# A recurrence in chunks of 64 tokens, its Gram products, triangular inverses and order rebuilt, ahead of a top-1 mixture of experts

## The chip, the cores and the metric

One core of one Trainium2 chip runs the whole program. The metric is the device time of one execution in microseconds. Before the change it is 550.36 us, the median of 3 runs (550.04 to 550.71).

The engines have one instruction stream each: TensorE (PE, matmuls), VectorE (DVE), ScalarE (ACT), GpSimd (POOL) and SyncE (SP, which only issues DMAs here). Each works through its stream in order and waits for the others at semaphores. PSUM banks take the products of TensorE, and ACT or DVE carry them on.

## The reference

Attention is a delta rule. For each of 4 batches and 8 heads a state of 48 by 48 runs over 768 tokens:

```python
k_n = k / (np.linalg.norm(k, axis=-1, keepdims=True) + 1e-06)
for t in range(S):
    kt, vt, bt = (k_n[:, :, t], v[:, :, t], beta[:, :, t, None])
    y[:, :, t] = np.einsum('bhd,bhde->bhe', q[:, :, t], state)
    v_old = np.einsum('bhde,bhd->bhe', state, kt)
    state = state + bt[:, :, :, None] * np.einsum('bhd,bhe->bhde', kt, vt - v_old)
```

Its output, as 3072 tokens of 384 numbers, goes through a mixture of 8 experts (384 to 1024 to 384):

```python
logits = x @ w_gate + modality_bias[modality_id]
e_idx = np.argmax(logits, axis=1)
# gate_w: the softmax of the chosen expert
h = np.maximum(x[mask] @ w1[e], 0.0)
out[mask] = gate_w[mask, None] * (h @ w2[e])
```

All is float32. The experts multiply float32 as a rounded high part and the rest, three products in place of one.

## The kernel before, in words

**Attention.** The 768 tokens are cut into 12 chunks of 64, the 32 batch-head pairs into two groups of 16, so there are 24 group steps i = 2c + g. Inside a chunk the recurrence is solved as a triangular system. Each step needs:

- the Gram products of its keys with its keys, and of its keys with its queries (method gram, L124). Keys are laid into a block-diagonal tile KB of 112 x 128, copied there by ACT and DVE, and 8 matmuls give four blocks of 32 keys and 64 queries each;
- the inverse of the triangular matrix. The 32 x 32 blocks on its diagonal are inverted for four steps at once, a set: 6 sets of 128 matrices, a matrix on each partition, by elimination: for each column a multiplication L213 and a subtraction L214, on DVE for the first 12 rows (sp1) and on POOL for the rest. Set 0 is done in blocks of 16, all on DVE, and joined by small products (jo, L247 and L253). Sets 0 and 1 stay on the chip; the others are carried through DRAM, both to bring blocks onto partitions and to bring the inverses back (R on L309, RTB on L305);
- level (L326, L330, L335, L338): the off-diagonal block of the inverse from two products, and the values scaled (L340, on POOL);
- chain: ks = state times keys (L363), RHS = values minus ks (L365, DVE), z = inverse times RHS (L378), ZT = z copied (ACT), state += keys times ZT (L386), Sbd = state copied (ACT), y = queries times state (L372) plus Gram times ZT (L394), xo = y copied (ACT), xd = xo written to DRAM (L397, SP);
- route: xo is transposed (L463), copied (L465) and multiplied by the gate's weights; each step writes 96 columns of one accumulating bank (L468).

Chain steps of one group follow on each other through the state; the two groups alternate.

**Routing and experts.** After 18 token tiles (step 17) part_a counts the tokens per expert, gives each a place (pt on TensorE, W, ranks, l0a and l1a one-hot tiles on DVE), sums the lists by matmuls (tpa) and copies them (tka, gidxa). SP reads the expert's number (sea) and loads its weights: w1 and w2 in four pieces each (w1ra, w2ra), which ACT rounds (w1ha, w2ha) and DVE takes the rest of (w1la, w2la). POOL gathers tokens from xd (xga), TensorE transposes them (xpa), ACT and DVE split them into x high and low. Layer 1 is hpa, layer 2 opa; POOL scatters the output rows (out_dram). The units in order are a0 to a3 (512 tokens each, from part_a's lists), b0 (512), c0 and c1 (256), e0 (128), whose lists part_b makes (tpb) from all 24 tiles. The order of all engines is found by the framework's scheduler from the written order and priorities, so a0's gather and first layer, and part_a, lie among steps 17 to 23.

## Time and profile before

| | before |
|---|---|
| median of 3 runs | 550.36 us |
| span of the profiled execution | 550.4 us |
| busy: PE, DVE, ACT, POOL | 483.5, 364.5, 263.5, 208.5 us |
| start of z of step 0, 4, 23 | 62.18, 131.68, 300.40 us |
| first product of a0's layer 1, of its layer 2 | 295.64, 317.71 us |
| start of the last scatter | 540.97 us |

The profiled execution's span is as long as a run, so its times can be set against the median as they are. Rows of a timeline have the start, the busy time (us), the engine, the line, the operation, output and input tiles and the count of instructions; in brackets the idle time ahead and what ended it. A float32 matmul shows as two records. PEclk is the clock that TensorE was granted, as a share of full speed.

### The profile page before, as it was taken

To read this page: it belongs to the slowest core of one execution; us is meant where nothing else is said; L and a number is where in the kernel's file an instruction comes from. 1 tells how busy PE (TensorE), PEld (TensorE's weight loads), DVE (VectorE), ACT (ScalarE), POOL (GpSimd) and SP (SyncE) were. 2 spreads that over 40 slices of the span, in tenths; PEclk is the share of its full clock that TensorE was granted. 3 is DMA by queue.
4 is the path that set the end of the run, shared out by engine and by line. 5 is a ranking of instruction groups with operands and counts; after the bars stand their busy time and mean duration, and the time that the engine had idled before them with its cause. 6 is when DMAs were issued, how large, how long until landed. Compare 5 with 4: busy or idle time off the path is not lost. (4 is left out here: it accounts for less than half of the span.)

```text
span 550.4 us, 14025 instructions
## 1 busy us (share of the span) xinstructions
PE 483.5 (88%) x5459; PEld 432.1 (79%) x5459; DVE 364.5 (66%) x877; ACT 263.5 (48%) x619; POOL 208.5 (38%) x350
## 2 busy tenths in 40 slices
...
GB/s 205 247 200 238 176 105 55 64 95 89 169 226 138 236 180 166 209 120 230 228 192 142 76 80 127 75 116 114 209 79 120 170 75 164 128 78 227 233 85 9
DMA packets 82716, 80.81 MB, mean 147 GB/s; under 512 B 50105, under 2 KB 73671, under 8 KB 81520
## 3 DMA queue, kind: packets, MB, share of 16 engines
...
q8 instruction: 45, 0.74, 0.6%
...
## 5 line engine op out<-in xcount | busy, mean ns | idle before, releaser
L733 PE MATMUL opa<-w2ha,h 128*128 128x384 f32 x256 | 69.1, 339 | 0.3 <-DVE ooa L736 0.3
L213 DVE TENSOR_TENSOR tm_x<-T,A 128x108 f32<-128x108 f32 (+12 forms) x165 | 57.8, 352 | 5.4 <-DVE PG L143 0.7
L124 PE MATMUL gp<-ke,KB 112*128 112x128 f32 x320 | 53.1, 331 | 9.3 <-DVE PG L143 3.9
L214 DVE TENSOR_TENSOR T<-T,tm_x 128x108 f32<-128x108 f32 (+12 forms) x165 | 56.8, 346 | 4.5
L124 PEld LDWEIGHTS gp<-ke,KB 112*128 112x128 f32 x320 | 48.3, 238 | 12.3 <-issue 3.7
L693 DVE SCALAR_TENSOR_TENSOR h<-hpa,h 128x512 fp32r<-128x512 f32 x32 | 22.0, 689 | 42.4 <-ACT h L692 42.4
L733 PEld LDWEIGHTS opa<-w2ha,h 128*128 128x128 f32 x256 | 46.2, 188 | 1.4 <-DVE ooa L736 0.5
L733 PE MATMUL opa<-w2la,h 128*128 128x384 f32 x128 | 43.0, 336 | 0.0
L692 ACT ACTIVATE h<-hpa 128x512 fp32r<-128x512 f32 x32 | 19.1, 596 | 49.5 <-PE hpa L690 49.5
L690 PE MATMUL hpa<-x,w1ha 128*128 128x512 f32 x144 | 39.1, 408 | 0.0
L340 POOL TENSOR_TENSOR kvn<-kvn,RR 128x384 f32<-128x384 f32 x22 | 18.7, 868 | 50.7 <-DMA kvn<-in_kv_dram 28.3
L363 PE MATMUL ks<-Sbd,kqr 112*64 112x96 f32 x352 | 27.3, 274 | 8.7 <-DMA kqr<-in_kq_dram 4.8
L365 DVE TENSOR_TENSOR RHS<-kvn,ks 64x384 f32<-64x384 f32 x44 | 24.2, 551 | 15.8 <-POOL kvn L340 9.4
L214 POOL TENSOR_TENSOR T<-T,tm_y 128x18 f32<-128x18 f32 (+8 forms) x90 | 30.7, 342 | 6.6
L213 POOL TENSOR_TENSOR tm_y<-T,A 128x18 f32<-128x18 f32 (+8 forms) x90 | 30.5, 339 | 6.6
L690 PEld LDWEIGHTS hpa<-x,w1ha 128*128 128x128 f32 x144 | 27.3, 194 | 5.5
L32 ACT COPY ZT<-z 64x384 f32<-64x384 f32 x48 | 22.7, 473 | 17.2 <-PE z L378 16.6
L363 PEld LDWEIGHTS ks<-Sbd,kqr 112*64 112x64 f32 x352 | 20.9, 150 | 11.8 <-ACT Sbd L32 4.4
L32 ACT COPY Sbd<-Sps 48x192 f32<-48x192 f32 x88 | 27.5, 313 | 5.2 <-PE Sps L386 2.7
L737 POOL DMA_INDIRECT out_dram<-ooa,sidxa x16 | 17.1, 1071 | 32.6 <-DMA out_dram<-ooa,sidxa 13.1
...
L378 PE MATMUL z<-RHS,R 128*64 128x96 f32 x384 | 26.9, 296 | 1.6 <-ACT R L338 1.6
...
## 6 DMA issues: line engine op xcount, KB each, us to landing
...
```

The costliest lines, as they stand in the source:

```text
L32: if n=="scalar": nc.scalar.copy(o,i)
L124: nc.tensor.matmul(gp[p][:,j,:],KB[:,x,:],k[:,x].rearrange("r a t -> r (a t)"),start=True,stop=True)
L213: yield I.tensor_tensor(o,y,z,ALU.mult)
L214: yield I.tensor_tensor(x,x,o,ALU.subtract)
L340: if c: E(C.vq).tensor_tensor(V,V,w,ALU.mult)
L363: nc.tensor.matmul(ks[64*p:64*p+64,:,j,:],KQ[:,4*p+j,0],hc(Sb[:,4*p+j,:]),start=True,stop=True)
L365: b=64*p; nc.vector.tensor_tensor(RH[b:b+64,:,48*p:48*p+48].rearrange("q (h j) c -> q h j c",h=2),VN[b:b+64],ks[b:b+64],ALU.subtract)
L378: s.PI['z',i]=nc.tensor.matmul(z[64*h:64*h+64,:,j,:],R[:,2*j+h,:],hc(RH[:,4*h+j,:]),start=True,stop=True)
L690: nc.tensor.matmul(hp[:,v,:],w[:,k,fs],x[:,k,0:T],start=(n==0),stop=(n==8)); n+=1
L692: nc.scalar.activation(hh,hp,AF.Relu)
L693: nc.vector.scalar_tensor_tensor(hl,hp,0.0,hh.bitcast(F32),ALU.max,ALU.subtract)
L733: mm=nc.tensor.matmul(op,h[:,f%nf,ts_],w[:,f%2,:],start=(n==0),stop=(n==23)); n+=1
```

## The change

- **Gram products in quadrants.** Keys and queries come without zeros, heads at partitions 0 and 64. A Gram of a chunk (both groups) is 32 matmuls of 48 rows, 64 columns out and 64 in (line 168), in all four quadrants of the array. Keys with keys (tiles gp0c, bank copies ev to gk) and keys with queries (gp1c, masked by DVE into pb) are two separate tasks. KB and its copies go, and the two matmuls at the start that multiplied nothing.
- **Set 0 first and in 16-blocks.** Its diagonal blocks are 32 x 32 products of their own (line 184) straight into a bank, then elimination of 15 columns on DVE as before, without key copies between.
- **Double sets.** JOBS is set 0, set 1, sets 2 and 3 together, sets 4 and 5 together. An instruction of a double job covers both sets (128 x 2 x ...). DVE has the first 8 rows of job 1 and the first 6 of jobs 2 and 3, POOL the rest; POOL also has the row scale and the final scale. Set 1 now goes through DRAM too, and the inverses come back by six small loads for each step from 4 on (rl, lines 348 and 351).
- **Logits by 32 columns.** The gate's weights are padded to 32 columns; for four tiles at once 12 matmuls give 32 rows each (line 529), ACT copies and DVE transposes.
- **xd is written by ACT's queue**, two DMAs a step.
- **Own list schedule.** The attention is a list of tasks with engine, duration, needs and buffers (class Plan). Latest times, backward from due times of z (T0 + PACE x i), are priorities; a simulation picks the order; in_order ties each engine to it.
- **Routing behind it.** part_a takes 20 tiles, is written after the whole attention, and a0's front and first layer may only issue after attention's last instruction on TensorE. List tiles come in rounds of 4 token tiles in place of 6. Expert buffers reuse those of the attention.

Three places in the instruction streams. First TensorE's start, the Grams of chunk 0's first step before:

```order
L124 MATMUL gp_0_122<-kqr_118,KB_112 128x128 [waits DMAHW0_49,DVE_49,Activation_49]
L124 MATMUL gp_0_122<-kqr_118,KB_112 128x128 x3
L124 MATMUL gp_1_127<-kqr_118,KB_112 128x128 x4
L124 MATMUL gp_1_150<-kqr_118,KB_113 128x128 [waits DMAHW1_49,Activation_49,Pool_49]
L124 MATMUL gp_1_150<-kqr_118,KB_113 128x128
```

and now, the diagonal blocks of step 2 and 3 and the Gram of chunk 0:

```order
L184 MATMUL S<-kqr_166 32x32 [waits DMAHW2_49]
L184 MATMUL S<-kqr_166 32x32 [waits DMAHW3_49]
L184 MATMUL S<-kqr_166 32x32 x62
L168 MATMUL gp_0_326<-kqr_165 64x64 x2
L168 MATMUL gp_1_327<-kqr_165 64x64 x2
```

The products no longer wait for copies by DVE and ACT, only for loads, and two matmuls to bank gp_0 alternate with two to gp_1.

Second, POOL ahead of the values of step 4 (kvn, now vv). Before, they stand among the rows of a single set:

```order
L213 TENSOR_TENSOR tm_y_1180<-T_1133,A_1132 128x70 [waits Pool_49]
L214 TENSOR_TENSOR T_1133<-T_1133,tm_y_1180 128x5x14 [waits Pool_49]
L340 TENSOR_TENSOR kvn_1823<-kvn_1823,RR_1841 128x384 [waits DMAHW1_49,Activation_49]
L340 TENSOR_TENSOR kvn_1823<-kvn_1823,RR_1841 128x384
L213 TENSOR_TENSOR tm_y_1186<-T_1133,A_1132 128x78 [waits Pool_49]
```

Now (T_1260 is job 2's tile):

```order
L312 TENSOR_TENSOR tmy_30_1981<-T_1260,A_950 128x2x24 [waits Pool_49]
L313 TENSOR_TENSOR T_1260<-T_1260,tmy_30_1981 128x2x24 [waits Pool_49]
L322 TENSOR_TENSOR T_1260<-T_1260,t_1173 128x1024 [waits DVE_49,Pool_49]
L322 TENSOR_TENSOR T_1260<-T_1260,t_1173 128x1024
L368 TENSOR_TENSOR vv_1376<-vv_1376,RR_1381 128x384 [waits DMAHW3_49,Activation_49]
L239 TENSOR_TENSOR A_1876<-A_1876,t_2043 128x1024 [waits DMAHW0_49,DMAHW5_49,DVE_49,Activation_49]
```

The values of step 4 moved behind the last row and the final scale of job 2.

Third, the copy of a0's list on DVE. Before, it stands behind the first of the four splits of w2:

```order
L675 TENSOR_TENSOR w2la_0_4803<-w2ra_0_4726,w2ha_0_4802 128x768 [waits DMAHW7_49,Activation_49]
L567 COPY tka<-tpa 128x16 [waits PE_49]
L569 COPY gatea<-tpa 128x16
L675 TENSOR_TENSOR w2la_1_4835<-w2ra_1_4728,w2ha_1_4834 128x768 [waits DMAHW0_49,Activation_49]
L568 TENSOR_SCALAR gidxa<-tka 128x16 [waits DVE_49]
```

Now it stands 31 rows behind the last of them, and part b's counts (names that end in b, c, e) lie between:

```order
L740 TENSOR_TENSOR w2la_3_5219<-w2ra_3_5064,w2ha_3_5218 128x768 [waits DMAHW7_49,Activation_49]
L634 TENSOR_TENSOR l1a<-l1a,tid 128x4x16 [waits DVE_49]
L567 TENSOR_TENSOR rt_4864<-rt_4864,OH 128x32 [waits DVE_49]
L588 TENSOR_REDUCE qfb<-cpb 128x8 [waits DVE_49]
...
L597 SCALAR_TENSOR_TENSOR Fnc<-qfc,Fnb 128x8 [waits DVE_49]
L637 COPY tka<-tpa 128x16 [waits PE_49]
L639 COPY gatea<-tpa 128x16
```

On TensorE pt, the counts of part_a, stand right behind the last logits (lg), and part b's first tpb ahead of a0's first xpa. The list copy moved behind all eight weight pieces.

The diff, cut to its core:

```diff
+RES=dict(mo=2,gp=1,ky=1); LEAD={}; T0=50; PACE=4.0; RATE=.28; AHEAD=3.0
+NKE=4; EKY=6; JOBS=((0,),(1,),(2,3),(4,5)); SPL=(0,8,6,6)
+EV=("ACT","DVE"); EV0=("ACT","DVE"); SCE="POOL"; RSE="POOL"; SBE=("ACT","ACT"); XE="ACT"
+NS=16; NE=8; NC=24
...
+                _,_,kind,t=heapq.heappop(events)
+                if kind=="ready": waiting.setdefault(t["eng"],[]).append(t)
+                elif kind=="give":
+                    for r,v in t["give"].items(): free[r]+=v
+            for e,w in waiting.items():
+                if busy.get(e,0)>now+1e-9 or not w: continue
+                w.sort(key=lambda t:(t["prio"],t["k"]))
+                for t in w:
+                    if all(free[r]>=v for r,v in t["take"].items()): break
+                else: continue
+                w.remove(t)
+                for r,v in t["take"].items(): free[r]-=v
+                t["start"]=now; end=now+t["dur"]; busy[e]=end; out.append(t); done=end
+                if t["mb"]:
+                    q=max(q,now+1.9)+t["mb"]/RATE; done=q
+                    if e=="SP": end=busy[e]=max(end,q-AHEAD)
+                t["end"]=end; n+=1; heapq.heappush(events,(end,len(T)+n,"free",t))
...
+def in_order(tc,first):
+
+    last={}
+    for i in tc.nc.cur_bb.bb.instructions[first:]:
+        e=i.engine
+        if isinstance(i,mybir.Instruction) and type(i).__name__.startswith('BassTile'): continue
+        if e in last: tc.add_manual_dep(i,last[e].name,mybir.DependencyInfo(mybir.DependencyClass.NoSync,mybir.DependencyReason.DATA),reason="order")
+        last[e]=i
+    return last
...
-        for h in range(2):
-            b=64*h
-            copy(nc,(C.kbe0 if i<C.kbp else C.kb1 if i<C.i0 else C.kbe)[h],KB[b:b+48,:,b:b+64],k[b:b+48,:,0])
-            for j in range(4):
-                x=4*p+j
-                nc.tensor.matmul(gp[p][:,j,:],KB[:,x,:],k[:,x].rearrange("r a t -> r (a t)"),start=True,stop=True)
+        def gram(c,a):
+            t=[s.mo(f"gp{a}{c}_{p}") if a or c%2==0 or c>=EKY else s.bank(f"gp{a}{c}_{p}",("ks","y")[p]) for p in range(2)]
+            for g in range(2):
+                for j in range(4):
+                    for p in range(2):
+                        for h in range(2):
+                            u=64*(h^p); x=4*p+j; l=s.KQ[c][u:u+48,g,x,0] if a else s.KE[c][u:u+48,g,x]
+                            mm(t[p][64*h:64*h+64,64*(4*g+j):64*(4*g+j)+64],l,s.KQ[c][u:u+48,g,x,1] if a else l,start=True,stop=True)
+            return t
...
+        def gpj(t,p): return t.rearrange("q (g p j) t -> q p g (j t)",g=2,p=2)[:,p]
+        def ev(c,p): cp(EV[p] if c>=4 else EV0[p],gpj(s.GC[c],p),s.gp[c][p].rearrange("q (g t) -> q g t",g=2))
+        def pg(c): s.pp[c]=gram(c,1); s.PB[c]=s.pk.tile([128,16,64],F32,name=f"pb{c}",tag="pb",bufs=2)
+        def pe(c,p):
+            for g in range(2): V.tensor_tensor(s.PB[c][:,8*g+4*p:8*g+4*p+4],s.pp[c][p][:,256*g:256*g+256].rearrange("q (j t) -> q j t",j=4),s.um.unsqueeze(1).to_broadcast([128,4,64]),ALU.mult)
+        def dg_(i):
+            k=s.KE[i//2][:,i%2]
...
-        if i in C.pml:
-            for h in range(2): nc.gpsimd.affine_select(out=P[64*h:64*h+64],in_=P[64*h:64*h+64],compare_op=ALU.is_gt,fill=0.0,base=0,pattern=[[0,8],[1,64]],channel_multiplier=-1)
...
-        st=([ops(0,B,V,"x",slice(k,k+1)) for k in range(2)] if C.ls else [ops(0,B,V,"x")]) if first else [ops(0,C.sp1,V,"x"),ops(C.sp1,32,nc.gpsimd,"y")]
+                def sub(J,n,c,lo,hi,e,nm):
+                    T=s.T[J]; X=s.A[J]; na=min(c,hi)-lo; nb=31-c; w=200 if nm=="x" else 160
+                    o=s.pa.tile([128,2,w],F32,name=f"tm{nm}{J}_{c}",tag="tm"+nm,bufs=2)[:,0:n,0:na*nb].rearrange("q k (a b) -> q k a b",a=na)
+                    E[e].tensor_tensor(o,T[:,:,lo:lo+na,c:c+1].to_broadcast([128,n,na,nb]),X[:,:,c:c+1,c+1:32].to_broadcast([128,n,na,nb]),ALU.mult)
+                    x=T[:,:,lo:lo+na,c+1:32]; E[e].tensor_tensor(x,x,o,ALU.subtract)
+                sp_=SPL[J]
+                for nm,e,lo,hi,f in (("x","DVE",0,sp_,dv),("y","POOL",sp_,32,po)):
+                    for c in range(lo+1,31):
+                        na=min(c,hi)-lo; d=2*f(n*na*(31-c))
+                        add(f"sub{nm}{J}_{c}",e,d,lambda J=J,n=n,c=c,lo=lo,hi=hi,e=e,nm=nm: sub(J,n,c,lo,hi,e,nm),[f"sub{nm}{J}_{c-1}"] if c>lo+1 else [f"ti{J}"],prio=pr)
...
+                def rd(J=J,sets=sets):
+                    for k,m in enumerate(sets):
+                        s.RD[m]=s.dr.tile([128,1024],F32,name=f"RD{m}",tag=f"RD{m}"); sp.dma_start(s.RD[m],s.Rb[J][:,k].rearrange("q a b -> q (a b)"))
...
+        def rld(i):
+            m,n=divmod(i,4)
+            for h in range(2):
+                q=64*h; sp.dma_start(s.RTB[i%2][q:q+32,:,32*h:32*h+32],bass.AP(tensor=s.RE[m].tensor,offset=s.RE[m].offset+(n*16+h)*1024,ap=[[32,32],[2048,8],[1,32]]))
+            for b in (1,0):
+                for p in range(2):
+                    q=64*p+32*b; sp.dma_start(s.R[i%4][q:q+32,:,32*b:32*b+32],bass.AP(tensor=s.RD[m].tensor,offset=s.RD[m].offset+(b*64+n*16+p*8)*1024,ap=[[32,32],[1024,8],[1,32]]))
...
-        copy(nc,C.yev,xo,y.rearrange("q h j c -> q (h j c)"))
-        s.XW=E(C.x_q).dma_start(s.xd[128*i:128*i+128],xo)
+        def xo(i): cp(XE,s.tile("xo",i,[128,2,192],3),s.y[i].rearrange("q h j c -> q h (j c)"))
+        def xd(i):
+            c,g=divmod(i,2)
+            for p in range(2): n=768*(2*g+p)+64*c; A.dma_start(s.xd[n:n+64],s.xo[i][64*p:64*p+64].rearrange("q h e -> q (h e)"))
...
-        for k in range(3): nc.tensor.matmul(s.lg[g][:,c0:c1,:],xs[:,k,:],s.wg[:,k,88-8*(c-c0):88+8*(c1-c)].rearrange("q (c e) -> q c e",e=8),start=False,stop=(k==2),skip_group_check=True)
+        def lg():
+            s.lg[u]=A.mo(f"lg{u}")[:,0:128]
+            for k in range(3):
+                for j in range(4): nc.tensor.matmul(s.lg[u][32*j:32*j+32],s.wg[:,k],A.xs[4*u+j][:,k],start=(k==0),stop=(k==2))
+        def le(): s.le[u]=A.pa.tile([128,128],F32,name=f"le{u}",tag="le"); nc.scalar.copy(s.le[u],s.lg[u])
+        def lt(): nc.vector.transpose(s.LT[:,4*u:4*u+4].rearrange("q b e -> q (b e)"),s.le[u])
...
+        p.add(f"xt{c}","PE",.36,xt,[f"xo{c}"],prio=c+1.5,take=dict(mo=1))
+        p.add(f"xs{c}","ACT",.5,xs,[f"xt{c}"]+([f"lg{u-1}"] if c>4 else []),prio=c+1.5,give=dict(mo=1))
+        if i==3:
+            p.add(f"lg{u}","PE",.7,lg,[f"xs{4*u+j}" for j in range(4)],prio=c+2,take=dict(mo=1))
+            p.add(f"le{u}","ACT",.27,le,[f"lg{u}"],prio=c+2,give=dict(mo=1))
+            p.add(f"lt{u}","DVE",.35,lt,[f"le{u}"],prio=c+2)
...
+            for i in range(H):
+                nc.tensor.matmul(tp.rearrange("q a b -> q (a b)"),A[:,i],B[:,i].rearrange("q a b -> q (a b)"),start=(h+i==0),stop=(h+i==t-1))
+        tk=T([128,NH],"tk"); V.tensor_copy(tk,tp[:,0])
+        V.tensor_scalar(gidx,tk,-1.0,0.0,ALU.add,ALU.max)
+        V.tensor_copy(gate,tp[:,1])
+        z=T([128,NH],"tz"); V.tensor_scalar(z,tk,0.0,8192.0,ALU.is_equal,ALU.mult)
+        V.tensor_tensor(sidx,gidx,z,ALU.add)
+
...
-        if i==2*C.cA-1:
-            with hp(C.hpa): R.part_a(pa,sea,prt,pm,"mo")
...
+    last=A.emit()
+    prt=ctx.enter_context(tc.tile_pool(name="prt",bufs=1))
+    sb=ctx.enter_context(tc.tile_pool(name="ea",bufs=1))
+    env=dict(sb=sb,sw=sb,w1=C.A1,w2=C.A2,ps=pm,xp="mo",xpb=2,hp="mo",hpb=2,op="mo",opb=2)
+    R.part_a(pa,sea,prt,pm,"mo")
+    R.rank(C.tA,24,prt,pm,"mo")
+    R.part_b(pb,seb,sec,see,prt,pm,"mo")
...
+    PE_=last[mybir.EngineType.PE]
+        if S is None:
+            with after(PE_,A.load.ins): S=X.front(*x,env)
+        S["env"]=env
+        with after(PE_) if n==0 else contextlib.nullcontext(): X.layer1(S)
```

864 lines of the change are left out of this document (408 added, 456 removed).

## The prediction

> **What bounds the kernel now.** I read the page first: busy shares, the 40 slices and the granted clock; then a table of stretches of 25 us; then TensorE's own timeline inside the stretches.
>
> ```profile
> PE 483.5 (88%) x5459; PEld 432.1 (79%) x5459; DVE 364.5 (66%) x877; ACT 263.5 (48%) x619; POOL 208.5 (38%) x350
> ...
> 75.00:100.00 25.00, 14.53 (x464) 12.90 (x464) 23.18 (x72) 9.19 (x27) 16.66 (x51) 0.74 0.17 45
> 100.00:125.00 25.00, 23.64 (x324) 20.57 (x324) 23.86 (x58) 14.15 (x41) 9.71 (x22) 0.72 0.35 88
> 125.00:150.00 25.00, 19.91 (x351) 16.97 (x343) 19.79 (x61) 15.53 (x42) 7.00 (x20) 0.90 0.41 123
> 150.00:175.00 25.00, 24.77 (x505) 21.50 (x505) 22.20 (x60) 16.55 (x44) 14.25 (x35) 0.97 0.72 191
> ...
> 350.00:525.00 175.00, 173.93 (x953) 160.06 (x953) 81.70 (x120) 66.51 (x104) 50.24 (x41) 0.98 0.44 137
> ```
>
> The columns are the stretch, its length, then busy time of PE, PEld, DVE, ACT and POOL, the granted clock, DMA share and GB/s. TensorE at 88% is an average over three stages. From 350 on the experts fill it (173.93 of 175). Before 125 VectorE is the full engine (23.18 and 23.86 of 25), TensorE has holes and its clock is 0.74 and 0.72. Between, TensorE is nearly full again, at the recurrence. How fast that goes is read from the starts of z (L378), one per group step:
>
> ```profile
> 62.18 0.88 PE L378 MATMUL z<-RHS,R 128*64 128x96 f32 x16 [0.93 <-ACT R L338]
> ...
> 131.68 0.43 PE L378 MATMUL z<-RHS,R 128*64 128x96 f32 x2
> ...
> 150.80 0.43 PE L378 MATMUL z<-RHS,R 128*64 128x96 f32 x2
> ...
> 231.45 0.88 PE L378 MATMUL z<-RHS,R 128*64 128x96 f32 x16
> 232.26 0.91 PE L468 MATMUL Sps<-wg,rxs 128*128 128x96 f32 x6
> 233.10 0.64 PE L326 MATMUL y<-RTB,PG 128*32 128x64 f32 x16
> ...
> 235.12 0.69 PE L335 MATMUL y<-R,ys 32*32 32x32 f32 x32
> 235.75 1.06 PE L363 MATMUL ks<-Sbd,kqr 112*64 112x96 f32 x15
> ...
> 237.96 0.88 PE L378 MATMUL z<-RHS,R 128*64 128x96 f32 x16
> ...
> 300.40 0.88 PE L378 MATMUL z<-RHS,R 128*64 128x96 f32 x16
> ```
>
> Step 0 is at 62.18, step 4 at 131.68, step 6 at 150.80, step 23 at 300.40. A step without a hole in TensorE is 237.96 - 231.45 = 6.51 us; the mean from step 6 to 16 (231.45) is (231.45 - 150.80)/10 = 8.07. So the recurrence costs a late start (131.68 for step 4), then 6.5 to 8 us a step. At the end it does not stand alone: a0's first layer runs between its steps.
>
> ```profile
> 252.41 0.24 DVE L489 COPY W<-pt 128x144 f32<-128x144 f32 x1
> ...
> 260.03 0.17 DVE L536 TENSOR_SCALAR sea<-sea 128x4 int32<-128x4 f32 x1
> ...
> 257.62 2.79 SPq L309 DMA_DIRECT2D R<-RD  x4
> ...
> 264.45 1.20 SPq L397 DMA_DIRECT2D xd<-xo  x1
> 266.74 2.12 SPq L646 DMA_DIRECT2D w1ra<-in_moe_w_dram  x4
> 269.58 1.68 SPq L305 DMA_DIRECT2D RTB<-RE  x2
> ...
> 271.97 0.83 ACT L674 CAST w1ha<-w1ra 128x768 fp32r<-128x768 f32 x1 [2.76 <-DMA w1ra<-in_moe_w_dram]
> ...
> 272.83 0.96 DVE L675 TENSOR_TENSOR w1la<-w1ra,w1ha 128x768 fp32r<-128x768 f32 x1 [7.33 <-ACT w1ha L674]
> ...
> 277.35 0.83 ACT L674 CAST w2ha<-w2ra 128x768 fp32r<-128x768 f32 x1
> ...
> 279.83 0.17 DVE L567 COPY tka<-tpa 128x16 f32<-128x16 f32 x1 [0.66 <-PE tpa L566]
> ...
> 295.64 1.67 PE L690 MATMUL hpa<-x,w1ha 128*128 128x512 f32 x6
> ...
> 297.85 1.56 PE L690 MATMUL hpa<-x,w1ha 128*128 128x512 f32 x6
> ...
> 299.95 0.30 PE L485 MATMUL pt<-OH,ones 128*128 128x32 f32 x2
> ...
> 317.71 0.59 PE L733 MATMUL opa<-w2ha,h 128*128 128x384 f32 x2
> ...
> 540.97 0.97 POOL L737 DMA_INDIRECT out_dram<-ooe,sidxb  x1 [6.57 <-DVE ooe L736]
> ```
>
> The routing of a0 (W at 252.41, list copied at 279.83, a0's first product at 295.64) takes over 43 us and is all under the recurrence.
>
> **The fixed end.** The span is 550.4 and the runs' median 550.36, so nothing lies outside the span and the sum is made against 550.4. From a0's second layer to the last scatter it is 540.97 - 317.71 = 223.3 us, of it 9.3 + 5.2 for part b's list:
>
> ```profile
> L566 PE MATMUL tpb<-l1b,l0b 128*128 128x88 f32 x48 | 9.3, 381 | 5.2 <-DVE l1b L564 5.2
> ```
>
> In the change that list stands ahead of a0's first layer (its cost comes with the gap below), so 223.3 - 14.5 = 208.8 stay. After the scatter's start 9.4 us remain. A block of layer 1 is 299.95 - 297.85 = 2.10, eight are 16.8. From a0's first product to the end: 16.8 + 208.8 + 9.4 = 235.0. Unit shapes and matmuls are the same on both sides, and the raw weights keep four buffers, so I cost the renamed buffers at nothing; their cover is TensorE's 99% in that stage.
>
> **When step 4 starts (z4).** Step 4 needs set 1 and its scaled values (vs4). In the written order of POOL vs4 stands behind all of job 1 (set 1) and all of job 2 (sets 2 and 3 together). So POOL's sum sets it:
>
> ```profile
> 26.68 0.52 DVE L213 TENSOR_TENSOR tm_x<-T,A 128x30 f32<-128x30 f32 x1
> ...
> 46.24 0.78 DVE L214 TENSOR_TENSOR T<-T,tm_x 128x30 f32<-128x30 f32 x1
> ...
> 62.12 1.26 POOL L195 TENSOR_SCALAR_AFFINE_SELECT T<-A 128x1024 f32<-128x1024 f32 x1 [4.83 <-DVE t L199]
> 63.47 0.22 POOL L213 TENSOR_TENSOR tm_y<-T,A 128x18 f32<-128x18 f32 x1
> ...
> 87.39 0.35 POOL L213 TENSOR_TENSOR tm_y<-T,A 128x90 f32<-128x90 f32 x1
> ...
> 119.04 1.91 POOL L340 TENSOR_TENSOR kvn<-kvn,RR 128x384 f32<-128x384 f32 x2
> ```
>
> Set 0's 30 operations took 26.68 to 47.0 because key copies stood between them and the small ones were 0.5 to 0.9; the copies go, so set 0 ends near 35 and job 1's row scales, a load later, near 43 (38 to 46). From 18 to 90 elements POOL's operation grows from 0.22 to 0.35, about 1.9 ns an element, and 384 elements take 0.95, which is the same line. With the 0.08 us between rows job 1's 44 operations (22 to 154 elements) come to about 20 us, job 2's 48 (48 to 312) to 33; a flatter slope, by the 1024 elements in 1.26, makes the second 24. Three scales and three final scales of 1024 elements, between 1.3 (L195) and 2.4 each (384 elements in 0.95, times 2.7), are some 11; three selects 4; copies of set 0's transposes 5. That is 64 to 73. So z4 is at 43 + 69 = 112, bounds 38 + 64 = 102 and 46 + 73 = 119, against 131.68.
>
> **What a step costs then.** From 6.51 I take out the wide logits (233.10 - 232.26 = 0.84 for 6 records of 96, 0.14 each) and put back a quarter of 12 matmuls, 24 records, in four column tiles. One after the other, at 0.14 x 128/96 each, they would be 4.5 us for four steps, 1.1 a step, and the gain turns into a loss of 0.3. But z's 16 records of 96, in two column tiles, take 232.26 - 231.45 = 0.81, 0.05 each, so tiles beside each other overlap; by that pace, and four tiles in place of two, 24 x 0.034 / 4 = 0.2 a step, which I take. The Grams of keys with queries are now made inside the loop, 64 records for two steps. No row has a 64 by 64 tile. L335 (32 by 32) is 32 records in 235.75 - 235.12 = 0.63, L326 (128 by 32) 16 in some 0.57: 64 records are 1.26 or 2.3. I take 1.26, since the four quadrants are nearest to L335, 0.63 a step. 6.51 - 0.84 + 0.20 + 0.63 = 6.50 with TensorE full. ACT has 16.55/25 x 8.07 = 5.3 us a step now; it gets the two issues of xd, some 0.4 each, and a Gram's mask stays with VectorE, so it is at 6.1. SP loses xd and gets six row loads a step: by 2.79/4 and 1.68/2 they are 2 x 0.84 + 4 x 0.70 = 4.5 us, with the chunk's other loads some 5.5. Both stay behind TensorE, by 0.4 and 1.0. Holes come on top: now 8.07 - 6.51 = 1.56 a step. The order is planned over all engines, so I take a quarter, 0.4: 6.9, bounds 6.1 (the small pieces at half their price, no hole) and 8.1 (the holes stay). Then z23 is at 112 + 19 x 6.9 = 243, and 7 us of ZT, pz, xo, transposes and logits later the recurrence ends: 250. The present last logits are still to come at z23's 300.40.
>
> [...]
>
> **What appears: an open gap.** All of part a stands behind the last logits on TensorE. From there, by the rows above: two counts and W 1.2; to the experts' numbers 260.2 - 252.4 less 1.7 for others' work, 6.1; the weight load issued 1.1 later at the least (264.45 + 1.20 to 266.74), 1.5; to its cast 5.2; low part 1.8, so 16. In the change tka, the copy of the finished list, stands on VectorE behind the last of w2's splits, w2la_3. From w1la's end (273.79) to w2's cast 277.35 and its split are 5.4, and three more loads at 1.15 each 3.5: 25. Some 25 small operations at 0.13: tka at 28. Then TensorE has part b's first tpb ahead of xpa: 40 operations with four of 480 elements and two of 512, 9.5 us, and after it 8 us of VectorE's l0b, l1b and x splits: a0's first product is 46 us after the last logits. Bounds 38 (the small ones overlap) and 54. TensorE idle that long starts slow; after the hole of 2.7 us z took nearly twice its time, and I add 2:
>
> ```profile
> 179.96 0.90 PE L463 MATMUL rxt<-ident,xo 128*128 128x128 f32 x3 [2.72 <-ACT R L338]
> 180.79 1.55 PE L378 MATMUL z<-RHS,R 128*64 128x96 f32 x16
> ```
>
> Sum: 250 + 46 + 2 + 235 = **533 us**. z23 comes 57 us earlier, but a0's first product, by this sum at 298, 2 us later than now (295.64): the open gap takes the recurrence's gain, and what is left is a first layer in one piece and part b's list out of the experts' way. It breaks even when recurrence and gap end at 550.4 - 237 = 313.4, so with this gap when the recurrence ends at 267.
>
> **The rivals.**
> A, the recurrence runs without holes and POOL on the flat slope: z4 at 104, steps of 6.2, end at 104 + 118 + 7 = 229, gap 42: 508. For it: the holes named above are waits on other engines' order. Against: every step of a written order waits for its slowest engine.
> B, slower than before: the holes stay. Each engine now has one fixed order, and SP's 5.5 us a step leave 1.0: where a row load is late, y1 waits, everything behind y1 on TensorE waits with it, TensorE's clock falls as at 179.96, and the step is 8.1 as now. Then z23 is at 112 + 19 x 8.1 = 266, the end at 273, and 273 + 46 + 237 = 556. It decides from a step of (267 - 7 - 112)/19 = 7.8 on. For it: 8.07 is what this trace has; against: DMA's share is 0.17 to 0.41 in 75 to 150, so there is room.
> C, a Gram goes at L326's pace, by pairs: 1.0 us more each, 24 of them, half of the first twelve hidden in the front: 533 + 18 = 551.
> D, POOL is slower still when VectorE works beside it, and job 2 ends at 130 as now: 533 + 18 = 551.
> E, the gap is longer than 54, for the four weight loads stand in one line with their splits: at 62 it is 549.
>
> **How the numbers follow.** Forecast 0.50, A 0.20, B 0.17, C 0.05, D 0.04, E 0.04. A time within 0.2% (1.1 us) of the one before counts as no change, about what a measurement of this kernel can tell. Faster: most of the forecast (0.48), A, and half of C, D and E (0.07): 0.75. Same: 0.04. Slower: B and the rest, 0.21. The range goes from A (508, a little under) to B: 504 to 557; the forecast's own is 518 to 546.
>
> **What would show it.** z4 near 112 with POOL full up to it; z starts 6.4 to 7.3 apart; Gram records near 1.3 us per 64; last logits near 250; TensorE empty for 46 us behind them, with tka behind w2la_3; 235 us from the first hpa to the end. Steps of 8, z4 at 130 or a gap of 60 would prove the forecast wrong.

## The result

The changed kernel takes 608.33 us (median of 4 runs, 607.31 to 614.21) against 550.54 us (4 runs, 550.04 to 551.82): a ratio of 1.107, 95% interval 1.101 to 1.113. It is slower by 58 us, where 533 was forecast. The profiled execution has a span of 605.6 us and a time of 607.43, so 1.8 us lie outside the span, which the forecast had put at nothing.

Set against the terms of the forecast, by the rows below:

| term | forecast | measured | miss |
|---|---|---|---|
| start of step 4's z | 112 | 157.94 | +46 |
| 19 steps to step 23's z | 19 x 6.9 = 131 | 155.4 (8.18 each) | +24 |
| that z to the end of the last logits | 7 | 9.3 | +2 |
| last logits to a0's first product | 46 + 2 | 47.8 | 0 |
| a0's first product to the end | 235.0 | 235.2 | 0 |

Two terms failed, and they hold 70 of the 72.6 us by which the span misses 533. The profile page's busy line and its instruction queue:

```profile
PE 449.8 (74%) x6863; PEld 403.3 (67%) x6863; DVE 315.4 (52%) x704; ACT 228.4 (38%) x480; POOL 224.8 (37%) x298
...
q8 instruction: 56, 0.92, 0.7%
```

Every engine but POOL is busy for less time than before (TensorE 449.8 against 483.5, VectorE 315.4 against 364.5), and TensorE has more instructions (6863 records against 5459). Less work in more time means waits. The table of stretches (PE, PEld, DVE, ACT, POOL, clock, DMA share, GB/s) says where:

```profile
75.00:100.00 25.00, 5.89 (x132) 4.52 (x128) 23.68 (x49) 4.23 (x13) 22.18 (x43) 0.64 0.10 32
100.00:125.00 25.00, 7.54 (x200) 6.41 (x203) 24.04 (x45) 2.66 (x4) 21.22 (x33) 0.50 0.18 30
...
400.00:575.00 175.00, 172.91 (x949) 158.93 (x948) 80.36 (x113) 67.88 (x106) 57.55 (x46) 1.00 0.45 140
```

From 75 to 125 VectorE is full again (23.68 and 24.04; before 23.18 and 23.86), with fewer instructions (49 and 45 against 72 and 58), POOL is now full beside it, and TensorE has 13.4 us of work in 50, where it had 38.2. In the experts nothing changed (172.91 of 175). TensorE's timeline at the points of the forecast:

```profile
114.53 1.97 PE L168 MATMUL gp<-ke 48*64 48x64 f32 x60 [32.90 <-DVE gk L26]
...
157.94 0.37 PE L397 MATMUL z<-RHS,R 128*64 128x96 f32 x1
...
166.49 0.88 PE L403 MATMUL S<-ZT,kk 128*48 128x96 f32 x8 [2.10 <-issue]
...
269.06 1.52 PE L403 MATMUL S<-ZT,kk 128*48 128x96 f32 x16 [4.67 <-ACT Sb L25]
...
311.50 1.16 PE L168 MATMUL gp<-kqr 48*64 48x64 f32 x64
...
313.30 0.83 PE L397 MATMUL z<-RHS,R 128*64 128x96 f32 x16
...
321.77 0.84 PE L529 MATMUL lg<-xs,wg 128*32 128x128 f32 x18 [0.76 <-ACT xs L525]
...
370.38 0.98 PE L755 MATMUL hpa<-xh,w1xa 128*128 128x512 f32 x3 [0.32 <-DVE xl L726]
```

The largest hole, 32.90 us, is a Gram that waits for VectorE's copy (gk) of the bank before it. In the steps TensorE waits for copies of the state (4.67), and sometimes for nothing recorded ("issue": 2.10, in the middle of a group of 16); such a wait is called a hole below.

What VectorE and POOL do in the meantime is the centre of this case. Each multiplication or subtraction of the elimination is called a row here. One of the same shape, 128 x 120, before:

```profile
91.97 0.37 DVE L213 TENSOR_TENSOR tm_x<-T,A 128x120 f32<-128x120 f32 x1
```

and in the change, with the other engines' rows around it:

```profile
35.40 12.81 SPq L192 DMA_DIRECT2D GD<-gk  x20
...
52.91 0.35 ACT L224 ACTIVATE s<-A,eps 128x32 f32<-128x32 f32 x1 [5.25 <-DMA A<-GD]
...
55.31 1.91 POOL L239 TENSOR_TENSOR A<-A,t 128x1024 f32<-128x1024 f32 x1 [19.89 <-DVE t L230]
...
88.50 0.52 DVE L312 TENSOR_TENSOR tmx<-T,A 128x120 f32<-128x120 f32 x1
...
109.93 0.43 DVE L313 TENSOR_TENSOR T<-T,tmx 128x264 f32<-128x264 f32 x1
...
111.22 2.38 POOL L322 TENSOR_TENSOR T<-T,t 128x1024 f32<-128x1024 f32 x1 [2.00 <-DVE T L313]
...
111.43 2.44 DVE L313 TENSOR_TENSOR T<-T,tmx 128x252 f32<-128x252 f32 x1
...
113.80 0.68 DVE L26 COPY gk<-gp 128x512 f32<-128x512 f32 x1
...
131.18 0.31 POOL L313 TENSOR_TENSOR T<-T,tmy 128x48 f32<-128x48 f32 x1
...
131.49 0.28 DVE L312 TENSOR_TENSOR tmx<-T,A 128x120 f32<-128x120 f32 x1
...
145.69 4.70 POOL L322 TENSOR_TENSOR T<-T,t 128x1024 f32<-128x1024 f32 x2 [14.20 <-DVE T L313]
```

While POOL works on its rows VectorE needs 0.52 for 120 elements; as soon as POOL's last row is done (131.49) it needs 0.28. Between 109.2 and 111.2 POOL is idle, and 264 elements take 0.43; then POOL's scale of 1024 elements starts (111.22, 2.38 us), and 252 elements take 2.44: VectorE's row ends (113.87) just behind POOL's instruction (113.60). By what means POOL's instruction holds VectorE's is not shown; what POOL's rows cost VectorE in all, e2 measures below. The trace also shows who waits on whom at the end: POOL's last scale stands 14.20 us for VectorE's rows, not the other way round.

### The profile page after: what moved, and what is told of

Read it like the earlier page. It is cut to its first block, busy times and chain, and to the rows that moved or that the text cites. A ratio compares the mean times of both kernels' runs of the same rounds, so it can differ in the third digit from the quotient of the medians.

```text
span 605.6 us, 16511 instructions
## 1 busy us (share of the span) xinstructions
PE 449.8 (74%) x6863; PEld 403.3 (67%) x6863; DVE 315.4 (52%) x704; ACT 228.4 (38%) x480; POOL 224.8 (37%) x298
## 4 chain that ended last, share of the span: by engine, by line
PE 54%; DVE 20%; DMA 9%; issue 5%; ACT 5%; SPq 3%; ACTq 1%; POOL 1%; POOLq 0%; DVEq 0%
PE hpa L755 11%; PE opa L798 10%; DVE T L313 5%; DVE tmx L312 4%; DMA kqr<-in_kq_dram 4%; PE hpc L755 3%; PE opc L798 3%; PE opb L798 3%; PE hpb L755 3%; PE gp L168 2%; PE ks L391 2%; PE y L411 2%; PE S L403 2%; PE z L397 2%; DMA A<-GD 2%
## 5 line engine op out<-in xcount | busy, mean ns | idle before, releaser
L393 DVE TENSOR_TENSOR RHS<-vv,ks 64x384 f32<-64x384 f32 x44 | 24.3, 551 | 82.5 <-issue 54.0
L755 PE MATMUL hpa<-xh,w1xa 128*128 128x512 f32 x192 | 53.7, 394 | 1.1 <-ACT xh L725 0.6
L313 DVE TENSOR_TENSOR T<-T,tmx 128x168 f32<-128x168 f32 (+27 forms) x90 | 47.9, 533 | 3.3
L368 POOL TENSOR_TENSOR vv<-vv,RR 128x384 f32<-128x384 f32 x22 | 18.9, 873 | 78.9 <-DMA vv<-in_kv_dram 51.5
L312 DVE TENSOR_TENSOR tmx<-T,A 128x168 f32<-128x168 f32 (+27 forms) x90 | 42.3, 470 | 7.1 <-POOL T L245 5.1
L313 POOL TENSOR_TENSOR T<-T,tmy 128x132 f32<-128x132 f32 (+19 forms) x70 | 39.6, 565 | 5.5
L755 PEld LDWEIGHTS hpa<-xh,w1xa 128*128 128x128 f32 x192 | 35.4, 188 | 7.7 <-ACT xh L725 0.8
L312 POOL TENSOR_TENSOR tmy<-T,A 128x132 f32<-128x132 f32 (+19 forms) x70 | 39.4, 563 | 3.0
L25 ACT COPY Sb<-S 48x192 f32<-48x192 f32 x88 | 27.5, 313 | 32.8 <-issue 11.6
L403 PE MATMUL S<-ZT,kk 128*48 128x96 f32 x352 | 22.3, 273 | 9.9 <-ACT Sb L25 5.9
L391 PE MATMUL ks<-Sb,kqr 112*64 112x96 f32 x352 | 23.4, 279 | 7.7 <-ACT Sb L25 6.4
```

Source lines behind the costliest of these rows:

```text
L25: if n=="scalar": nc.scalar.copy(o,i)
L312: E[e].tensor_tensor(o,T[:,:,lo:lo+na,c:c+1].to_broadcast([128,n,na,nb]),X[:,:,c:c+1,c+1:32].to_broadcast([128,n,na,nb]),ALU.mult)
L313: x=T[:,:,lo:lo+na,c+1:32]; E[e].tensor_tensor(x,x,o,ALU.subtract)
L368: if c: G.tensor_tensor(v,v,w,ALU.mult)
L391: for p in range(2): mm(s.ks[i][64*p:64*p+64,:,j,:],s.KQ[c][:,g,4*p+j,0],hc(s.Sb[g][:,4*p+j,:]),start=True,stop=True)
L393: c,g=divmod(i,2); b=64*p; V.tensor_tensor(s.RHS[g][b:b+64,:,48*p:48*p+48].rearrange("q (h j) c -> q h j c",h=2),s.KV[c,1][b:b+64,g],s.ks[ ...
```

## The experiments

The times of the experiments are single executions, beside 549.87 to 553.51 for the kernel before. Differences below some 7 us are not told apart by them (the changed kernel's own times spread over 7); the starts of z say more. Per step is (step 23's z less step 4's) / 19. Records and holes (in us) are TensorE's matmul records and its waits put down to "issue" between 165 and 315 us. The steps of the kernel before have a0's first layer among them.

| kernel | time | z of step 4 | per step | records | holes, us |
|---|---|---|---|---|---|
| before | 550.5 | 131.7 | 8.88 | 2210 | 1.4 |
| the change | 608.3 | 157.9 | 8.18 | 3076 | 13.3 |
| e1 Gram copies on ACT | 597.0 | 148.6 | 8.10 | 3014 | 14.0 |
| e2 no POOL rows | 592.4 | 143.8 | 8.18 | 2888 | 10.4 |
| e3 no row loads | 607.6 | 162.1 | 7.99 | 3186 | 18.3 |
| e4 planner's costs as measured | 612.6 | 160.8 | 8.20 | 2900 | 7.6 |
| e5 single sets | 602.8 | 136.7 | 8.98 | 2912 | 0.6 |
| e6 xd on SP | 601.9 | 153.7 | 8.21 | 2997 | 5.8 |
| e7 values first | 610.8 | 159.8 | 8.29 | 3001 | 14.8 |
| e8 = e5 + e6 + e1 | 576.7 | 125.0 | 8.39 | 2683 | 3.4 |
| e9 all rows on VectorE | 609.3 | 152.2 | 8.64 | 2852 | 9.8 |
| e10 = e9 + xd on POOL + e1 | 604.4 | 158.9 | 7.87 | 3086 | 18.9 |
| e11 routing among the steps | 617.6 | 161.6 | 8.12 | 3118 | 17.1 |
| e12 = e8 + e11 | 593.9 | 127.8 | 8.60 | 2719 | 2.7 |
| e13 = e10, wide query Grams | 595.9 | 158.5 | 7.35 | 2800 | 8.9 |

**The front: what makes step 4 late.** First the copy that TensorE waits 32.90 us for, moved to ACT with the order unchanged:

```diff
-        def ev(c,p): cp(EV[p] if c>=4 else EV0[p],gpj(s.GC[c],p),s.gp[c][p].rearrange("q (g t) -> q g t",g=2))
+        def ev(c,p): cp("ACT" if c>=4 else EV0[p],gpj(s.GC[c],p),s.gp[c][p].rearrange("q (g t) -> q g t",g=2))
```

> The Gram copies of chunks 4 to 11 that stood on VectorE are made by ACT; the order is held. Theory H (a Gram on TensorE waits for its copy, which stands on VectorE behind the rows of jobs 1 and 2, and everything behind that Gram waits with it): the hole of 33 us from 81 to 114 is gone, step 2 starts near 90 to 100 in place of 131.9. If H also sets step 4, step 4 comes to 115 and the time to about 565. Theory D (VectorE's rows, each slowed while POOL works, end job 2 at 145 whatever TensorE does, and POOL's values of step 4 stand behind job 2): step 4 stays at 150 to 158 and the time at 597 to 606.

The hole did not close; it moved four Grams on, in TensorE's timeline of this kernel:

```profile
81.03 1.15 PE L168 MATMUL gp<-ke 48*64 48x64 f32 x60 [0.53 <-ACT gk L25]
...
125.97 0.48 PE L168 MATMUL gp<-kqr 48*64 48x64 f32 x4 [34.80 <-DVE pb L177]
```

Now the mask of a Gram of keys with queries, also behind VectorE's rows, is what TensorE stands for, 34.80 us. Step 4 came 9 us earlier, at 148.6 (150 to 158 expected by theory D), the time was 597.01. So it is not one copy: whatever TensorE needs from VectorE next stands behind the same rows.

The second run leaves out the computation of POOL's rows (rows from 8 on in job 1 and from 6 on in the others are not eliminated there); everything else stays:

```diff
                     o=s.pa.tile([128,2,w],F32,name=f"tm{nm}{J}_{c}",tag="tm"+nm,bufs=2)[:,0:n,0:na*nb].rearrange("q k (a b) -> q k a b",a=na)
+                    if e=="POOL": return
```

> POOL's row operations of jobs 1 to 3 are left out, so the inverses of sets 1 to 5 are not right; everything else stands in the same order. Theory D: VectorE's rows fall from a mean of 0.53 us to 0.32 (0.165 us + 1.04 ns an element), job 2's rows end near 105 to 110 in place of 145, step 4 starts near 118, the time is near 560 to 568. If VectorE's rows are slow by themselves they stay at 0.5, job 2 ends near 140 and the time is over 590.

The same 180 instructions of VectorE, by groups (count, busy time, mean ns), in the change with POOL's rows under them, and then without POOL's rows:

```profile
L313 DVE TENSOR_TENSOR T<-T,tmx 128x168 f32<-128x168 f32 (+27 forms) x90 | 47.9, 533 | 3.3
...
L312 DVE TENSOR_TENSOR tmx<-T,A 128x168 f32<-128x168 f32 (+27 forms) x90 | 42.3, 470 | 7.1 <-POOL T L245 5.1
L313 POOL TENSOR_TENSOR T<-T,tmy 128x132 f32<-128x132 f32 (+19 forms) x70 | 39.6, 565 | 5.5
L312 POOL TENSOR_TENSOR tmy<-T,A 128x132 f32<-128x132 f32 (+19 forms) x70 | 39.4, 563 | 3.0
```

```profile
L314 DVE TENSOR_TENSOR T<-T,tmx 128x168 f32<-128x168 f32 (+27 forms) x90 | 31.3, 348 | 3.3
L313 DVE TENSOR_TENSOR tmx<-T,A 128x168 f32<-128x168 f32 (+27 forms) x90 | 28.8, 320 | 7.1 <-POOL T L245 5.1
```

VectorE's rows fall from 90.2 to 60.1 us. POOL's 79.0 us of rows cost VectorE 30.1. But job 2's last row ended at 131.3 and not at 105 to 110, step 4 came at 143.8 (14 us earlier) and not at 118, and the time was 592.35 and not 560 to 568. So slow rows are only a part of the delay. Another part stands in the change's own trace, ahead of step 3:

```profile
139.46 1.13 ACTq L418 DMA_DIRECT2D xd<-xo  x2
...
141.65 1.72 PE L391 MATMUL ks<-Sb,kqr 112*64 112x96 f32 x15 [6.35 <-ACT Sb L25]
...
143.57 1.12 DVE L393 TENSOR_TENSOR RHS<-vv,ks 64x384 f32<-64x384 f32 x2 [7.72 <-PE ks L391]
```

ACT stands idle for 8.01 us ahead of its copies of the state (Sb), because the issue of xd ahead of them waits for a semaphore that one of SP's loads for job 3 sets when it lands, at 139.39. TensorE waits for Sb, VectorE for ks, and the last four rows of job 2 stand behind that on VectorE. Without POOL's rows the same chain held TensorE for 8.42 us; e6 below takes it away.

The counterpart computes everything, with all rows on VectorE (the tasks that read the constants' tile also wait for its load here):

```diff
-NKE=4; EKY=6; JOBS=((0,),(1,),(2,3),(4,5)); SPL=(0,8,6,6)
+NKE=4; EKY=6; JOBS=((0,),(1,),(2,3),(4,5)); SPL=(0,31,31,31)
...
-                    T=s.T[J]; X=s.A[J]; na=min(c,hi)-lo; nb=31-c; w=200 if nm=="x" else 160
+                    T=s.T[J]; X=s.A[J]; na=min(c,hi)-lo; nb=31-c; w=256
```

> Edit: all 31 columns' rows of jobs 1 to 3 are VectorE's (no row of the solution on POOL); nothing else moved. Theory R (beside POOL's wide rows a VectorE row costs 0.53 us, alone about 0.28 to 0.37, so POOL's half buys nothing): the rows of the three jobs take VectorE about 22 + 33 + 33 = 88 us at 0.22 + 1.04 ns per element, about what they take now (90), and nothing waits for POOL's sum; step 4's z at 140 to 165 against 157.9, the time within 15 us of 608. Rival (two engines do more than one even so): VectorE needs as long for each row as now with twice the rows, step 4's z at 195 or later, the time 640 or more. Steps unchanged at 8.0 to 8.4 by both.

```profile
L312 DVE TENSOR_TENSOR tmx<-T,A 128x168 f32<-128x168 f32 (+25 forms) x90 | 50.0, 555 | 1.8
L313 DVE TENSOR_TENSOR T<-T,tmx 128x168 f32<-128x168 f32 (+25 forms) x90 | 49.7, 552 | 3.4
```

All rows alone cost VectorE 99.7 us, its part of them beside POOL 90.2. That is above the 88 expected, but POOL's 79 us of work save VectorE only 9.5. The time is the same within what a single execution tells (609.25), step 4 is 6 us earlier. So POOL's part of the double sets bought next to nothing (the order was planned anew with the new split, which is a second difference between the two runs).

Was the order at fault, since the planner reckons each engine as if it were alone (0.165 us and 1.04 ns an element on VectorE, 0.25 and 1.15 on POOL)? It was given what the change's trace shows:

```diff
-        dv=lambda n: .165+n*1.04e-3
-        po=lambda n: .25+n*1.15e-3
+        dv=lambda n: .25+n*2.1e-3
+        po=lambda n: .28+n*2.1e-3
...
-            else: add(f"gd{c}","SP",1.6,lambda c=c: gd(c),[f"ev{c}_0",f"ev{c}_1"],mb=.52)
+            else: add(f"gd{c}","SP",2.6,lambda c=c: gd(c),[f"ev{c}_0",f"ev{c}_1"],mb=.52)
```

> Only numbers of the planner change: a row on VectorE 0.25 us + 2.1 ns an element in place of 0.165 + 1.04, on POOL 0.28 + 2.1 in place of 0.25 + 1.15 (lines through this case's 156 and 130 row operations with their gaps), a Gram's writes 2.6 us of SP in place of 1.6. Theory O (the order was made from durations that do not hold beside each other, so the wrong things stand in front): step 4 starts near 135 to 140, the time is 575 to 590. Theory D alone: VectorE and POOL have the same work, step 4 stays near 150 to 158 and the time within 5 us of 606.

Step 4's z 160.8, the time 612.57: no gain. A better-informed order of the same work did not help here, where one engine is full. And the step of the forecast by which POOL's place for the values decides when step 4 starts, with the values of steps 4 and 5 (vs4, vs5) moved right behind job 1's final scale (rs1):

```diff
-        for t in s.ordered(p): t["fn"]()
+        o=s.ordered(p); v=[t for t in o if t["name"] in ("vs4","vs5")]; o=[t for t in o if t not in v]
+        k=o.index(p.at["rs1"])+1
+        for t in o[:k]+v+o[k:]: t["fn"]()
```

> POOL scales the values of steps 4 and 5 right behind job 1's final scale, ahead of the rest of job 2; nothing else moves. By the forecast's own step (POOL's order holds step 4 until job 2 is through): step 4 starts at 138 to 145 in place of 157.9, right behind step 3, and the time is 590 to 597. If VectorE's order holds it (RHS of steps 2 and 3 behind the rows of job 2), step 4 moves by less than 5 us and the time by less than 6.

Step 4's z 159.8, the time 610.79. The values were ready some 36 us sooner, and step 4 was as late as before: the values' place on POOL does not hold it. But the end of job 2 still did, by another engine. ACT's copy of job 2's inverses needs POOL's final scale, and step 4's ys stands behind that copy on ACT:

```profile
152.86 3.74 ACT L325 COPY A<-T 64x1024 f32<-64x1024 f32 x2
...
157.44 1.06 PE L363 MATMUL lv<-R,ys 32*32 32x32 f32 x32 [2.75 <-ACT ys L358]
```

The same pair stands in the change (3.73 and 2.74). No run moves this copy, so what it costs by itself is open.

Single sets, with the old split of 12 and 20 rows:

```diff
-NKE=4; EKY=6; JOBS=((0,),(1,),(2,3),(4,5)); SPL=(0,8,6,6)
+NKE=4; EKY=6; JOBS=((0,),(1,),(2,),(3,),(4,),(5,)); SPL=(0,12,12,12,12,12)
```

> The double jobs are undone: six jobs of one set, VectorE with the first 12 rows as in the kernel before, POOL with 20; the order is planned anew. Theory W (POOL's operations on two sets, up to 312 elements, slow VectorE's, and set 1 waits for set 3): VectorE's rows return to a mean near 0.33 us, step 4 starts at 115 to 130, the time is 565 to 580. If the front is slow for another reason (VectorE's order, SP's writes), step 4 stays at 145 to 158 and the time above 592. The steps after it are not touched and stay at 8 us.

Step 4 came 21 us earlier (136.7), and the steps went up to 8.98: VectorE has 242 row instructions, 95.4 us, between 55 and 220, so the rows no longer stand in one block ahead of step 4 but between the steps. The time was 602.82. Nearly all of the gain in the front is paid back. Step 4 also came later than theory W said (115 to 130), and VectorE's rows have a mean of 0.39 us, not 0.33.

**The steps.** The rival B of the forecast had late row loads. From step 8 on they were left out (the steps then use old inverses):

```diff
         def rld(i):
+            if i>=8: return
```

> The six row loads a step are left out from step 8 on (the steps then use the inverses of set 1, which is not the right result). Theory L (SP's queue, where each load waits for the one eight before it to land, sets the step): from step 8 the steps go at 6.4 to 6.8 us, step 23 starts 20 to 25 us earlier and the time is 580 to 588. If the holes come from the written order of the other engines the steps stay at 8 and the time above 600.

The same 150 us in the change, and then without the row loads:

```profile
165.00:315.00 150.00, 125.39 (x3076) 109.11 (x3077) 64.84 (x131) 86.95 (x225) 47.56 (x60) 0.91 0.71 145
```

```profile
165.00:315.00 150.00, 127.96 (x3186) 111.81 (x3186) 68.85 (x141) 88.64 (x229) 50.98 (x69) 0.91 0.54 128
```

DMA's share in these 150 us fell to 0.54 from 0.71, and the steps went from 8.18 to 7.99, the time to 607.58. The row loads are not what a step mainly waits for, and a lower load of the DMA engines did not make the holes smaller (18.3 us here).

ACT issues xd itself, and a late issue holds what stands behind it. In the change:

```profile
264.34 3.02 ACTq L418 DMA_DIRECT2D xd<-xo  x2
...
267.40 0.96 ACT L25 COPY ZT<-z 64x384 f32<-64x384 f32 x2 [7.47 <-DMA xd<-xo]
```

Each of the two issues went out as soon as a load of SP's had landed (264.26 and 266.85); the next ZT copy came after 7.47 us of idle time, and TensorE stood for Sb (269.06 above). The two issues were given to SP:

```diff
-            for p in range(2): n=768*(2*g+p)+64*c; A.dma_start(s.xd[n:n+64],s.xo[i][64*p:64*p+64].rearrange("q h e -> q (h e)"))
+            for p in range(2): n=768*(2*g+p)+64*c; sp.dma_start(s.xd[n:n+64],s.xo[i][64*p:64*p+64].rearrange("q h e -> q (h e)"))
```

> The two writes of xd a step are issued by SP in place of ACT; all orders are held. Theory X (ACT stands still when the issue of xd waits for an earlier transfer to land, and ZT and Sb of the chain stand behind it): ACT's waits on DMA go, the holes of 4.7 us ahead of the state product go, the steps from 4 to 23 fall from 8.2 to 7.4 to 7.8 us and the time to 590 to 598. If SP's own queue then becomes the bound (five loads and two writes a step), the steps stay at 8 or grow and the time is 604 to 620.

```profile
PE ks L391 <- DMA kqr<-in_kq_dram: 14.4, 6, 5.1
```

The waits for ACT went, in the front too: step 3's z follows step 2's by 5.6 us in place of 14.5. But TensorE now stood 14.4 us for the loads of keys and queries, which SP issues behind xd. A step stayed at 8.21; the time was 601.87, and step 4's z came 4 us earlier, which is most of the gain. Single sets (e5), xd on SP and the Gram copies on ACT (e1) together, by the three diffs shown:

> Three edits together: single sets, xd on SP, Gram copies of chunks 4 to 11 by ACT. If their causes are apart from each other the gains add: single sets some 30, ACT's copies 8, xd 10, so 555 to 565. If they cover for the same wait (VectorE at the front, SP in the steps) it is 570 to 585.

The time was 576.74, inside the range for causes that cover for each other, and yet a gain of 31.6 us, more than the three single gains add up to (11.3 + 5.5 + 6.5). VectorE in this kernel, by stretches:

```profile
75.00:100.00 25.00, 17.54 (x378) 15.27 (x380) 23.12 (x67) 11.16 (x26) 16.73 (x41) 1.00 0.49 111
...
200.00:225.00 25.00, 21.66 (x558) 18.86 (x555) 23.47 (x57) 16.76 (x42) 10.93 (x21) 0.93 0.84 192
```

Step 4 is at 125.0, ahead of the kernel before, but VectorE is at 21 to 23 of 25 in every stretch until 225 save one (18.4 from 175 to 200), and a step takes 8.39.

Then xd on POOL, which has little else to do in the steps when all rows are VectorE's (18.7 of 150 us in e9), and the Gram copies on ACT (e1):

```diff
-            for p in range(2): n=768*(2*g+p)+64*c; A.dma_start(s.xd[n:n+64],s.xo[i][64*p:64*p+64].rearrange("q h e -> q (h e)"))
+            for p in range(2): n=768*(2*g+p)+64*c; G.dma_start(s.xd[n:n+64],s.xo[i][64*p:64*p+64].rearrange("q h e -> q (h e)"))
```

> As the run before, with two edits for the steps: the DMA issues of each chunk's output (xd) on POOL's queue, which has nothing else to do in the recurrence, and Gram copies of chunks 4 to 11 on ACT. Theory X (a step takes 8.2 and not 6.9 because ACT stands behind its own DMA issues for xd, and what ACT copies for the step comes late): z 6.9 to 7.3 apart after step 4, so 19 steps 131 to 139 instead of 155; the time 18 to 25 below the run before. Rival H (the steps are held by holes inside groups of matmuls, in which the engine waits for nothing recorded, and by the slow clock after them): 7.9 to 8.4 apart as before, the time within 6 of the run before. Rival Q (PE then stands at its own next load, as when xd went on SP): waits on kqr of 10 us or more in the window of the steps.

```profile
PE y L411 <- issue: 5.6, 2, 5.2
PE S L403 <- issue: 5.6, 2, 4.5
PE lv L363 <- issue: 4.3, 2, 2.7
PE y L414 <- issue: 3.0, 2, 1.8
PE lv L363 <- ACT ys L358: 1.5, 3, 1.0
PE ks L391 <- DMA kqr<-in_kq_dram: 1.5, 1, 1.5
```

All waits for other engines are small now, the time is 604.43, and a step from step 10 on still takes 7.93; VectorE's rows end at 211, and from step 12 (219.36) to 23 (308.32) it is 8.09. What is left are the holes inside groups of matmuls, 18.9 us in 150, and a clock of 0.93 in that window. So ACT's issues were a real wait, and behind it stood another; theory X (6.9 to 7.3) is wrong and H (7.9 to 8.4) right, at its lower end.

What are the holes, then? Their distances in the change, counted in all of TensorE's instructions (matmuls, weight loads and a few of its sequencer), are 1535, 513, 768, 768, 1279 and 768: multiples of 256 within one. The queue q8 brings TensorE's instructions in packets of 16384 bytes, 56 of them for 13897 instructions, 248 to a packet.

The trace has a time for each packet too, and they fit the holes one by one. The seven holes in the change's 150 us, with the landing of the packet that belongs to the boundary:

| hole, from and to | packet landed | then until TensorE goes on |
|---|---|---|
| 164.39 to 166.49 | 165.14 | 1.3 |
| 203.75 to 204.20 | 202.88 | 1.3 |
| 213.19 to 216.31 | 214.90 | 1.4 |
| 232.68 to 234.87 | 233.44 | 1.4 |
| 250.38 to 252.06 | 250.76 | 1.3 |
| 282.24 to 283.96 | 282.46 | 1.5 |
| 298.97 to 301.08 | 299.59 | 1.5 |

Over the whole traces of all 15 kernels 158 of 163 holes stand at the same place of the 256 (the 193rd or 194th), and each of the 158 ends 1.2 to 1.9 us behind the landing of its packet. At the 623 other boundaries the packet had landed in time, at 538 of them 2 us and more ahead. So TensorE stands in these holes because its next instructions are not there yet. What delays a packet, no run here asks. The last run on the steps asks whether fewer records make the holes smaller. On top of e10, each Gram of keys with queries is made by 32 records of 128 columns (the second of each pair of tiles gets its neighbour's keys):

```diff
+                for j in range(0,4,2) if a else ():
+                    for p in range(2):
+                        for h in range(2):
+                            u=64*(h^p); x=4*p+j; mm(t[p][64*h:64*h+64,64*(4*g+j):64*(4*g+j)+128].rearrange("q (x t) -> q x t",x=2),s.KQ[c][u:u+48,g,x,0],s.KQ[c][u:u+48,g,x:x+2,1],start=True,stop=True)
-                for j in range(4):
+                for j in () if a else range(4):
```

> Edit: all rows on VectorE, xd on POOL's queue, Gram copies on ACT (the run of 604.43), and each Gram of keys with queries made by 32 records of 128 columns instead of 64 of 64 (the second tile of each pair gets its neighbour's keys, so its values are not the reference's; the work per step on every other engine is the same). Theory I (the holes inside groups of matmuls are TensorE running out of instructions: 20.5 records per us of step leave 18.5 us of them between 165 and 315, 19.4 leave 0.6, 17.9 leave 3.6, and before's 14.7 leave 1.4): at 17 to 18 records per us the holes in that window fall from 18.5 to under 6, and z is 7.0 to 7.5 apart from step 10 on instead of 7.93; the time 592 to 598. Rival H2 (the holes come from something else, a DMA or the clock gate): 12 us of holes or more, 7.8 or more a step, the time within 5 of 604.

```profile
PE lg L533 <- issue: 3.5, 1, 3.5
...
PE lv L359 <- issue: 3.1, 1, 3.1
PE lv L367 <- issue: 2.3, 1, 2.3
```

Holes 8.9 us against 18.9, from step 10 on 7.51 a step against 7.93 (from step 12 on 7.33 against 8.09), the time 595.93 against 604.43. The direction is theory I's, and the time falls where it said; the records (18.7 per us, 17 to 18 expected), the holes (under 6 expected) and the step (7.0 to 7.5) miss it a little. The table of kernels has the same trend, from 2210 records and 1.4 us of holes to 3186 and 18.3, though with exceptions (e5 has 2912 records and 0.6 us): what counts is whether the packet is in time, and the count of records is only a part of that. That the holes are missing instructions is shown by the landings; how many us a given count of records costs is not, with a single execution of each kernel.

**The open gap.** Its size was forecast right, and so was its inside: tka was to come 28 us behind the last logits and comes 27.6 behind their end at 322.61.

```profile
350.21 0.17 DVE L637 COPY tka<-tpa 128x16 f32<-128x16 f32 x1
```

Whether its place was the price, e11 asks. part_a is written behind the logits of tile 19 and left out of the attention's fixed order, part_b behind a0's first layer:

```diff
-        for t in s.ordered(p): t["fn"]()
+        L=s.nc.cur_bb.bb.instructions; skip=set()
+        for t in s.ordered(p):
+            t["fn"]()
+            if t["name"]=="lt4":
+                k=len(L); s.hook(); skip.update(range(k,len(L)))
...
+    A.hook=lambda: R.part_a(pa,sea,prt,pm,"mo")
...
-    R.part_a(pa,sea,prt,pm,"mo")
-    R.rank(C.tA,24,prt,pm,"mo")
-    R.part_b(pb,seb,sec,see,prt,pm,"mo")
...
         with after(PE_) if n==0 else contextlib.nullcontext(): X.layer1(S)
+        if n==0:
+            R.rank(C.tA,24,prt,pm,"mo"); R.part_b(pb,seb,sec,see,prt,pm,"mo")
```

> Edit: the changed kernel with part_a written right behind the logits of tile 19 (no longer behind the whole attention, and not tied to its order; its list sum goes into free columns of the bank of the states, its tiles into Gram buffers that are free by then), and part_b written behind a0's first layer instead of ahead of it. Theory G (the open gap is the price of this order, as forecast): the counts of part a fall to step 20, a0's weights and list are ready 15 to 25 earlier against the last logits, the gap of 47.8 shrinks to 22 to 33; z23 stays at 313 within 4 and the stage behind a0's first product lengthens by at most 12 for part b's list: the time 585 to 600. Rival W (the gap is a0's weight loads and splits, which must wait for buffers of the attention's last chunks): the gap stays above 40 and the time above 602.

```profile
325.67 0.84 PE L534 MATMUL lg<-xs,wg 128*32 128x128 f32 x18 [0.75 <-ACT xs L530]
...
357.30 1.65 PE L760 MATMUL hpa<-xh,w1xa 128*128 128x512 f32 x3 [0.57 <-ACT xh L730]
...
391.46 1.98 PE L641 MATMUL tpb<-l1b,l0b 128*128 128x88 f32 x8 [14.58 <-DVE l1b L639]
```

The gap fell from 47.8 to 357.30 - 326.51 = 30.8, inside the expected 22 to 33, and the time rose to 617.64. Behind a0's first product the kernel takes 615.9 - 357.3 = 258.6, 23 more: part b's counts and lists, on VectorE, begin only when they may, and TensorE's first tpb, placed ahead of a0's second layer, waits 14.58 for them; with the list's own products (7.1) that is 21.7 of the 23. The expected limit of 12 was too low. Part b's chain has to lie under something long; ahead of a0's first product it lay in the gap that was open anyway. On top of the best version:

> The routing of the run before together with single sets, chunk outputs issued by SP and Gram copies on ACT (the edits that together gave 576.74). Theory (the terms are independent and add): 576.7 less what the run before gains over 608.3, which by theory G is 8 to 23: 553 to 569; so even with all four parts undone or moved the kernel is not below 550.5, because a step still takes 8.4. Rival (VectorE has little room up to step 14 and the routing works beside it later, so the two gains overlap): 570 or more.

593.86 against 576.74 for e8: the gap is 31.1 there and 258.0 follow it. So both expected sums failed by the same term, and no version tried comes below the kernel before.

## Why the prediction was wrong, step by step

- **"So POOL's sum sets it" (112, measured 157.94).** This is the step that failed most. The sum itself was right: from its first scale (55.31) to the end of step 4's values (151.2) POOL is busy for 67.7 us, and 69 was taken. But it stands idle for another 28.2 in between, 16.2 of them for VectorE's rows, and the forecast had put POOL's waits at nothing. It gave VectorE no price at all, though the quoted table had it at 23 to 24 of 25 in the same stretch. Beside POOL's rows, now twice as wide, a VectorE row of 120 elements costs 0.52 where it cost 0.37; e2 puts that at 30 us of VectorE's time, e9 shows that the split gains only 9.5. POOL's last row of job 2 ends at 131.5, VectorE's at 145.5, though 7.72 us of that difference is VectorE waiting behind ACT's issue of xd, a second wait that the forecast did not have. e7 shows that the values' place on POOL was not the bound. The single runs win 4 to 21 us of the 46 (e1, e2, e5, e6, e9), and e8 33 together, so no one of these causes is the whole. Rival D, "POOL is slower still when VectorE works beside it", named the mechanism from POOL's side alone; it had a chance of 0.04 and a price of 18.
- **"Set 0 ends near 35 and job 1's row scales ... near 43".** Set 0's rows end at 42.3, and job 1's scale starts at 55.31. Its set comes through DRAM, and the load was written on SP behind 20 writes that took until 48.2. This is 12 of the 46.
- **"It is a quarter, 0.4" for the holes of a step (6.9, measured 8.18).** With TensorE full, 6.50 is nearly borne out: from 165 to 315 it is busy 125.39 of 150 at a clock of 0.91, 6.84 a step. The rest, 1.34, was to be 0.4. Of these idle 24.6 us 13.3 are holes in which TensorE's instructions had not arrived, 0.73 a step; the kernel before has 1.4 us of them in the same 150. The others are waits for ACT behind its own DMA issues, for VectorE and for the loads (e6, e10). The wrong ground was that a planned order takes holes away; the planner knows neither of instructions that arrive late nor of issues that wait.
- **Rival B, slower with steps of 8.1,** had the step right and the mechanism wrong (e3: without the row loads a step still takes 7.99). Its time, 556, was too low, since it kept step 4 at 112.
- **Rival C.** A Gram's 64 records take 1.16 us at a granted clock of 1.00 (311.50); 1.26 was taken, and 2.3 would have been L326's pace. At a clock of 0.50, 60 records take 1.97 (114.53).
- **The gap (46 + 2, measured 47.8) and the end (235.0, measured 235.2)** were right, by the mechanism too (tka 27.6 behind the last logits; the granted clock was 0.57 from 322.7 to 370.3, and what that cost by itself no run shows). By the break-even, recurrence and gap had to end by 313.4; they end at 370.4, 57 later, which is the loss.
- **The range** took the bad end of one term at a time. Both at once (step 4 at 119, steps of 8.1) would have given 563, still 45 short, since the upper bound of 119 left VectorE out.
